# A three-stage kernel on one core: where the attention scores stand among a tile's products, and which banks hold its tables and state products

## The chip, the core and the metric

The kernel runs on one core of one Trainium2 chip. Five engines work side by side, each through its own list of instructions in order: TensorE (PE; its weight loads are PEld in the profile), VectorE (DVE), ScalarE (ACT), GpSimd (POOL) and SyncE (SP), which here issues most of the DMAs. An instruction starts when its engine has finished the one ahead of it and when the semaphores that it waits for have been raised. The metric is the device time of one execution in microseconds (us); the median of a few runs is compared.

## What is computed

Three stages follow each other: a linear attention with a decaying state, a mixture of eight experts with one expert per token, and a dense layer pair with x - tanh(x) between.

```python
def _attn_ref(r, k, v, w, u):                     # B,H,S,D = 4, 8, 768, 48
    for t in range(S):
        cur = einsum('bhd,bhe->bhde', u * k[t], v[t])
        y[t] = einsum('bhd,bhde->bhe', r[t], state + cur)
        state = w * state + einsum('bhd,bhe->bhde', k[t], v[t])

def _moe_ref(x, w_gate, w1, w2):                  # N=3072, D=384, E=8, F=1024
    probs = softmax(x @ w_gate); e = argmax(x @ w_gate)
    out = probs[e] * (relu(x @ w1[e]) @ w2[e])    # per token

def _moe2_ref(x, w_in, w_out):                    # 384 -> 2048 -> 384
    h = x @ w_in
    return (h - tanh(h)) @ w_out
```

## The kernel before

**Attention, tile by tile.** The 768 steps are cut into 6 chunks c of 128 steps; with 4 batches b this gives 24 tiles, `seq = [(c, b), ...]`, numbered n = 0 to 23. A tile holds 8 heads of 48, as 4 pairs j of two heads q. For one tile the kernel does:

- `load`: two DMAs on SP bring `n_b[n % 5]` (r, k, v by step, 576 KB) and `t_b[n % 5]` (r and k by dimension, 384 KB). There are five buffers of each, so the loads of tile n+5 wait until tile n has been used up.
- `side`: POOL makes `rk` = r*k, `rku` = rk*u and `kh` (k times a table).
- `diag_sum`: DVE sums `rku` over a head into `dt`; `diag`: ACT writes eight 128x128 diagonal matrices from it into the tile `am`.
- `scale`: DVE multiplies both halves of `t_b` by powers of the decay, one table for each half. The first, `PRKp[0]`, lies in PSUM (tag K). The second, `PRKp[1]`, lies in PSUM (tag X) for the first four tiles; `scale_rows` copies it to the SBUF tile `PRK1`, and later tiles read it there.
- `scores`: PE multiplies k and r into two banks, `A0` and `A1`, of which there is one each. `mask`: DVE copies the causal part from the banks into `am`.
- `outp`: PE multiplies r with the state of the chunk before (the **state part**, L418), adds `am` times v (the **v part**, L423) in `yh0` and `yh1`, and ACT copies both to `y`.
- `state_mm`: PE makes the state products into `Pp`, a part of the bank `yh2`; `state_add`: DVE adds them to the decayed state (`sw`, POOL), L402. Neither is needed in the last chunk.

**The gate** follows some tiles behind, once for each chunk of four: `logits` and `logits2` (PE), `gate` (nine small DVE operations and one ACT exponential), `rank_mm`, `rank_of`, `rank_in`, `rank_q`, `rank_row`, `idx_mm`: they find each token's expert and its place. Their small results share one PSUM bank, `sm`. `at_step(n, first, fn)` runs `fn` for a chunk `first` steps after the tile number that ends it. **The output** `xout(n - 7)` transposes a finished tile on PE into the bank X, scales it on ACT (`xout_g`) and writes it to `xd` in DRAM by SP; `XOUT` changes this for the last steps.

**The order** is written out by hand in the loop over n, and every engine's list follows it. In step n stand: loads of tile n+3, `diag_sum(n+1)`, `scale(n+1)`, `logits`, the output of an older tile, `outp(n-1)`, `state_mm(n)`, `diag(n+1)`, `scores(n)`, `mask(n)`, `state_add(n)`, `side(n+2)`, and the gate's parts. So scores(n) stand behind the v part of tile n-1 on PE, and on SP the loads of step n+1 stand behind the write to `xd` of step n.

**After the loop.** For the tokens of the first expert a head start is made: `head_gather` (POOL, step 22) fetches 256 rows of `xd` by an index list, as soon as the outputs of tiles 0 to 15 have landed there; `head_trans` (L610) is the first PE work after the loop's last v part, and from there on PE goes through the experts' products and the dense stage. The kernel's first lines of the loop that matter here:

```python
            if 1 <= n <= NN:
                outp(n - 1)
                at_step(n, 6, rank_row)
            if n > 1 and n < NN:
                state_mm(n)
```

Of the kernel before, what the change touches and what calls it, by code (L numbers as in the profile page):

```python
# [30 lines left out]
def rwkv_moe_moe_kernel(ctx: ExitStack, tc: tile.TileContext, rk_t, rkv, pk, u, wp1, wp2, out):  # L31


    nc = tc.nc
# [175 lines left out]
    PRK1 = ap_.tile([PT, HP, P], F32, name="PRK1")  # L210
# [7 lines left out]
    Pb = yh[2]  # L218
    Pp = Pb[:, 0:HP * D].rearrange("p (j d) -> p j d", d=D)
# [139 lines left out]
    def diag(n):  # L359
        dt = st.pop(("dt", n))  # L360
        am = at3.tile([P, 2, HP, P], F32, tag="am", name="am")
        for h in range(H):
            nc.scalar.activation(out=am[:, h % 2, h // 2, :], in_=ident, func=ACTF.Copy, scale=dt[:, h:h + 1])  # L363
        st["am", n] = am
# [43 lines left out]
    def outp(n):  # L408
        c, b = seq[n]
        am = st.pop(("am", n))  # L410

        if c > 0:
            for i in range(2):
                for g in range(2):
                    for q in range(2):
                        rows = slice(64, PT) if q else slice(0, 64)
                        j, p0 = 2 * i + g, 64 * g
                        nc.tensor.matmul(Yp[q][p0:p0 + D, i, :], lhsT=Sc[c % 2][b][rows, j, :],  # L418
                                         rhs=t_b[n % NB][rows, 0, j, :], start=(i == 0), stop=False)
        for q in range(2):  # L420
# [18 lines left out]
    PRKp = [ps1.tile([P, HP, P], F32, tag=tag, name=f"prk{tag}")[0:PT] for tag in "KX"]  # L439
# [23 lines left out]
    def gate(c):  # L463

# [5 lines left out]
        ex = exs[c % 2]  # L470
        nc.scalar.activation(out=ex[:, :, 0:E], in_=sh, func=ACTF.Exp)
        ssum = gp.tile([P, B], F32, tag="ssum", name="ssum")
        gt = gp.tile([P, B], F32, tag="gt", name="gt")
        nc.vector.scalar_tensor_tensor(out=scp, in0=sh, scalar=0.0,
# [4 lines left out]
        nc.vector.tensor_reduce(out=ssum, in_=ex, axis=AX.X, op=ALU.add)  # L479
        oh = OH[:, c]  # L480
        nc.vector.tensor_tensor(out=oh, in0=scp, in1=bc(mx.unsqueeze(2), [P, B, E]), op=ALU.is_equal)
        nc.vector.reciprocal(out=gt, in_=ssum)
        st["gt", c] = gt
        nc.vector.tensor_reduce(out=s4p, in_=oh.rearrange("p b e -> p e b"), axis=AX.X, op=ALU.add)
        nc.vector.tensor_tensor(out=cum[c + 1], in0=cum[c], in1=s4p, op=ALU.add)
        if H0 <= c < C - 1:
            nc.vector.tensor_tensor(out=cums[c + 1 - H0], in0=cum[c + 1], in1=bump16, op=ALU.add)

# [97 lines left out]
    def keep_warm(k):  # L586

        for _ in range(k):
            nc.tensor.matmul(yb[2][:, 3 * P:], lhsT=ident, rhs=ident, start=True, stop=True)
# [119 lines left out]
    with tc.manual_schedule():  # L709
# [44 lines left out]
        XOUT = {NN - 3: (NN - 10, NN - 9), NN - 2: (), NN - 1: (NN - 8, NN - 7), NN: ()}  # L754
        for n in range(NN + 1):
# [14 lines left out]
            with_logits = n % B == 1 and n > B  # L770
# [7 lines left out]
            if n > 1 and n < NN:  # L778
                state_mm(n)
            if xs_of and with_logits:  # L780
                xout_t(xs_of[0])
            if xs_of:
                xout_g(xs_of[0])
            if 0 < n < NN - 1:
                diag(n + 1)
            if n < NN:
                scores(n)
                for m in xs_of[1:]:
                    xout_t(m)
                    xout_g(m)  # L790
                mask(n)
                if n == 0:
                    k_rows()
                    diag(1)
                elif n == 1:
                    state(0)
                    state(1)
                else:
                    state_add(n)
# [6 lines left out]
            at_step(n, 3, logits2)  # L806
            at_step(n, 3, gate)
            at_step(n, 6, idx_mm)
            if n == H0 * B + 3:
                head_count()  # L810
            at_step(n, 4, rank_mm)
            at_step(n, 4, rank_of)
            at_step(n, 5, rank_in)
            if n == H0 * B + 3:
                head_end()
# [5 lines left out]
            if n == 1:  # L821
                scale_rows()
# [689 lines left out]
```

## Time and profile before

| | |
|---|---|
| time, median of 3 runs | 772.89 us (771.71 to 773.98) |
| the profiled execution's own time | 772.78 us |
| its span, first to last instruction | 771.1 us |
| PE busy in the span | 755.7 us (98%) |
| DVE busy | 639.2 us (83%) |
| ACT busy | 509.1 us (66%) |
| POOL busy | 430.9 us (56%) |

The attention loop takes about the first 118 us of the span, the rest belongs to the experts and the dense layers. A busy share says how much of a stretch had an instruction of that engine running; it doesn't say what the engine would need at its fastest, and for PE, whose matmuls overlap, it is the starts of consecutive groups that tell how long a group holds the engine.

### The profile page before, as it was taken

The numbers are of one execution on the slowest core, as the hardware profiler recorded it, in microseconds if no ns is written. First come the engines' busy times: TensorE is split into PE (matmuls) and PEld (weight loads), VectorE is DVE, ScalarE is ACT, GpSimd is POOL, SyncE is SP. The second block draws the span as 40 slices with busy tenths as digits, with TensorE's granted clock in tenths as the row PEclk, the third lists the DMA queues.
The fourth block names the chain that finished last, engine by engine and source line by source line (L and its number), as shares of the span: only waits on it lengthen the run. The fifth ranks groups of instructions, "written<-read, shape, count | busy, mean of one in ns | idle before, by whom it ended". The sixth has DMA issues, their size and how long they took to land.

```text
span 771.1 us, 14624 instructions
## 1 busy us (share of the span) xinstructions
PE 755.7 (98%) x5200; PEld 684.6 (89%) x5200; DVE 639.2 (83%) x1155; ACT 509.1 (66%) x1091; POOL 430.9 (56%) x435
## 2 busy tenths in 40 slices
PE   8899989999999999999999999999999999999997
PEld 7688868998999999999898998989989989899887
DVE  7899996788899888964898888888888888888893
ACT  6788885464454445554887766776777677677881
POOL 6989952385877876765355353443534344343433
PEclk9999999999999999999999999999999999999999
DMA  8999945466999899974000010000001000000101
GB/s 238 261 291 290 318 128 167 145 189 201 256 230 271 223 305 286 250 198 144 1 1 0 1 42 1 0 21 21 1 1 42 1 1 24 18 1 1 41 1 42
DMA packets 34656, 89.67 MB, mean 116 GB/s; under 512 B 5499, under 2 KB 12704, under 8 KB 34578
## 3 DMA queue, kind: packets, MB, share of 16 engines
q1 hardware_dynamic: 30384, 78.68, 34.8%
q0 software_dynamic: 4192, 9.99, 4.6%
q8 instruction: 43, 0.70, 0.4%
q14 instruction: 35, 0.29, 0.1%
q10 hardware_dynamic: 2, 0.00, 0.0%
HBM read 72.92 MB, written 15.74 MB: 115 GB/s over the span
## 4 chain that ended last, share of the span: by engine, by line
PE 51%; issue 2%; ACT 1%; POOL 1%; POOLq 0%
PE h L1346 25%; PE o L1394 24%; PE y L1119 1%; PE hps L1094 1%; POOL out_dram L1407 0%; PE o L1346 0%; POOL g L1383 0%; POOLq L1453 0%; POOL xb L1383 0%; ACT s L1354 0%; ACT mk L1356 0%; POOLq L1507 0%; ACT xb L1382 0%; ACT z L1350 0%; ACT t L1352 0%
## 5 line engine op out<-in xcount | busy, mean ns | idle before, releaser
L1383 POOL TENSOR_TENSOR g<-t,g 128x512 fp32r<-128x512 f32 x93 | 120.3, 1294 | 178.6 <-ACT g L1382 128.5
L1346 PE MATMUL h<-xb,ring 128*128 128x512 f32 x855 | 213.6, 395 | 0.0
L1394 PE MATMUL o<-ring,g 128*128 128x384 f32 x1116 | 209.3, 336 | 0.0
L1394 PEld LDWEIGHTS o<-ring,g 128*128 128x128 f32 x1116 | 196.1, 188 | 8.2
L1346 PEld LDWEIGHTS h<-xb,ring 128*128 128x128 f32 x855 | 159.7, 188 | 30.5
L85 POOL TENSOR_TENSOR ring<-stg,ring 128x384 fp32r<-128x384 f32 x102 | 105.3, 1053 | 53.8 <-ACT ring L84 42.4
L1350 ACT ACTIVATE z<-h 128x512 f32<-128x512 f32 x95 | 56.9, 599 | 95.2 <-PE h L1346 95.2
L1119 PE MATMUL y<-h,ring 128*128 128x256 f32 (+7 forms) x576 | 114.2, 342 | 0.6 <-DVE h L1098 0.6
L1094 PE MATMUL hps<-xt,ring 128*128 128x472 f32 (+6 forms) x504 | 105.6, 353 | 0.1
L1119 PEld LDWEIGHTS y<-h,ring 128*128 128x128 f32 x576 | 101.3, 188 | 4.1 <-DVE h L1098 1.0
L1362 DVE TENSOR_TENSOR t<-t,h 128x512 f32<-128x512 f32 x95 | 65.1, 685 | 41.3 <-ACT t L1352 40.9
L1094 PEld LDWEIGHTS hps<-xt,ring 128*128 128x128 f32 x504 | 90.6, 188 | 3.7 <-DVEq L1233 0.4
L1367 DVE COPY_PREDICATED t<-mk,h 128x512 f32<-128x512 uint32 x95 | 71.4, 751 | 10.1 <-DVE h L1365 0.5
L84 ACT CAST ring<-stg 128x384 fp32r<-128x384 f32 x152 | 70.2, 512 | 9.5 <-DMA stg<-in_wp_dram 8.9
L1364 DVE SCALAR_TENSOR_TENSOR h<-s,h 128x512 f32<-128x512 f32 x95 | 66.2, 697 | 10.6 <-ACT g L1382 0.9
L1097 ACT ACTIVATE h<-hps 128x256 fp32r<-128x256 f32 (+7 forms) x64 | 32.1, 501 | 63.8 <-PE hps L1094 61.8
L1354 ACT ACTIVATE s<-z,gb 128x512 f32<-128x512 f32 x96 | 69.6, 725 | 0.0
L1356 ACT ACTIVATE mk<-z,gt 128x512 f32<-128x512 f32 x96 | 69.3, 721 | 0.0
L1365 DVE SCALAR_TENSOR_TENSOR h<-z,h 128x512 f32<-128x512 f32 x95 | 66.1, 696 | 3.3
L1363 DVE TENSOR_TENSOR h<-h,z 128x512 f32<-128x512 f32 x95 | 65.9, 693 | 0.0
L1382 ACT CAST g<-t 128x512 fp32r<-128x512 f32 x93 | 57.6, 619 | 9.7 <-DVE t L1367 7.8
L363 ACT ACTIVATE am<-ident,dt 128x128 f32<-128x128 f32 x192 | 58.6, 392 | 3.8 <-DVE dt L356 3.8
(254 smaller groups left out, 1039.6 us busy)
## 6 DMA issues: line engine op xcount, KB each, us to landing
stg<-in_wp_dram SPq DMA_DIRECT2D x64, 384.0 KB, 4.9
n<-in_rkv_dram SPq DMA_DIRECT2D x24, 576.0 KB, 6.0
d<-in_wp_dram SPq DMA_DIRECT2D x32, 384.0 KB, 5.8
t<-in_rk_t_dram SPq DMA_DIRECT2D x24, 384.0 KB, 7.1
wdec<-dcf SPq DMA_DIRECT2D x32, 192.0 KB, 5.3
xd<-xs SPq DMA_DIRECT2D x24, 192.0 KB, 3.9
stg<-wdec SPq DMA_DIRECT2D x12, 384.0 KB, 4.3
wl<-wdec SPq DMA_DIRECT2D x2, 768.0 KB, 6.0
```

Source lines behind the costliest of these rows:

```text
L84: nc.scalar.copy(out=dst[:, 0, sl], in_=of)
L85: eng.tensor_tensor(out=dst[:, 1, sl], in0=of, in1=dst[:, 0, sl].bitcast(F32), op=ALU.subtract)
L1094: nc.tensor.matmul(ps, lhsT=wf(a, kk), rhs=xt[e][b][:, kk, :], start=(n == 0), stop=(n == 8))
L1119: nc.tensor.matmul(yps[d], lhsT=wf(a)[:, d * P:(d + 1) * P], rhs=h2[:, b, :], start=(f == 0 and n == 0), stop=(f == CH1 - 1 and n == 2))
L1346: nc.tensor.matmul(ps, lhsT=wf(a, kk), rhs=xb[j][:, b, kk, :], start=(n == 0), stop=(n == 8))
L1354: nc.scalar.activation(out=s, in_=z, func=ACTF.Square, scale=G_K ** 0.5, bias=gb)
L1356: nc.scalar.activation(out=mk, in_=z, func=ACTF.Relu, scale=-1.0, bias=gt2)
L1364: nc.vector.scalar_tensor_tensor(out=ps, in0=s, scalar=G_K * G_D, in1=ps, op0=ALU.add, op1=ALU.mult)
L1365: nc.vector.scalar_tensor_tensor(out=ps, in0=z, scalar=G_A, in1=ps, op0=ALU.subtract, op1=ALU.mult)
L1367: nc.vector.copy_predicated(out=t, mask=mk.bitcast(U32), data=ps)
L1383: nc.gpsimd.tensor_tensor(out=g[:, 1, :], in0=ww, in1=g[:, 0, :].bitcast(F32), op=ALU.subtract)
L1394: nc.tensor.matmul(ops[q], lhsT=gg[i][:, b, q * P:(q + 1) * P], rhs=wf(a), start=(f == 0 and n == 0), stop=(f == CH2 - 1 and n == 2))
```

## The change

1. Both decay tables stay in PSUM: `PRKp[1]` moves to the bank `yb[2]` (`yh2`), `PRK1` and `scale_rows` go, and `scale` reads `PRKp[k]` for all tiles.
2. The state products `Pp` move from `yh2` to free columns (304 to 496) of `sm`, the bank of the gate.
3. `outp` is split. In step n PE now does the state part of tile n-1, then scores(n), then the gate's products, then the v part of tile n-1, then the state products, then the output's transposes.
4. `diag` is split: five of the eight diagonal matrices ahead of the copies of `y`, three behind. The output of the older tile goes to the end of the step.
5. `gate` is split so that its order on DVE differs (the sum and reciprocal last), and the outputs of tiles 13 to 17 are spread over other steps (`XOUT`).
6. The products that keep PE busy at the start write to the bank X.

```diff
-    PRK1 = ap_.tile([PT, HP, P], F32, name="PRK1")
...
-        for k, by in enumerate((PRKp[0], PRKp[1] if n < B else PRK1)):
-            nc.vector.tensor_tensor(out=t[:, k], in0=t[:, k], in1=by, op=ALU.mult)
-
-    def scale_rows():
-        nc.scalar.copy(out=PRK1, in_=PRKp[1])
+        for k in range(2):
+            nc.vector.tensor_tensor(out=t[:, k], in0=t[:, k], in1=PRKp[k], op=ALU.mult)
...
+    def diag(n, part=range(H)):
+        if 0 in part:
+            st["am", n] = at3.tile([P, 2, HP, P], F32, tag="am", name="am")
+        dt, am = st["dt", n], st["am", n]
+        for q, j in (divmod(k, HP) for k in part):
+            h = 2 * j + q
+            nc.scalar.activation(out=am[:, q, j, :], in_=ident, func=ACTF.Copy, scale=dt[:, h:h + 1])
...
+    PRKp = [t.rearrange("p (j t) -> p j t", t=P)[0:PT] for t in (ps1.tile([P, BANK], F32, tag="K", name="prk"), yb[2])]
+    Pp = sm[:, 304:304 + HP * D].rearrange("p (j d) -> p j d", d=D)
...
-        XOUT = {NN - 3: (NN - 10, NN - 9), NN - 2: (), NN - 1: (NN - 8, NN - 7), NN: ()}
+        XOUT = {NN - 4: (NN - 11, NN - 10), NN - 3: (NN - 9,), NN - 2: (), NN - 1: (NN - 8, NN - 7), NN: ()}
...
-            at_step(n, 2, logits)
...
-            if xs_of and not with_logits:
-                xout_t(xs_of[0])
-            if 1 <= n <= NN:
+            ahead = range(1, NN - 1)
+            if n:
+                outp_state(n - 1)
+            if n < NN:
+                scores(n)
+                mask(n)
+            if n in ahead:
+                diag(n + 1, range(5))
+            at_step(n, 2, logits)
+            at_step(n, 3, logits2)
+            if n == H0 * B + 3:
+                head_count()
+            at_step(n, 4, rank_mm)
+            for m in xs_of[1:]:
+                xout_t(m)
+                xout_g(m)
+            if n:
                 outp(n - 1)
                 at_step(n, 6, rank_row)
...
+            if n in ahead:
+                diag(n + 1, range(5, H))
...
+            elif n < NN:
+                state(n)
+            at_step(n, 3, gate_top)
+            at_step(n, 3, gate_exp)
+            at_step(n, 3, gate_sum)
+            at_step(n, 4, rank_of)
+            at_step(n, 5, rank_in)
...
+            for m in xs_of[:1]:
+                xout_t(m)
+                xout_g(m)
```

PE, in step 14: before, the end of tile 13's state part (L418), its v part (L423), the state products of tile 14 (L390) and the first of its scores (L372).

```order
L418 MATMUL yh_162<-t_128,Sc_148 48x128
L423 MATMUL yh_161<-am,n_133 48x128 x4
L423 MATMUL yh_162<-am,n_133 48x128 x4
L390 MATMUL yh_163<-n_134,kh_160 64x48
L390 MATMUL yh_163<-n_134,kh_160 48x48
L390 MATMUL yh_163<-n_134,kh_160 64x48
L390 MATMUL yh_163<-n_134,kh_160 48x48
L390 MATMUL yh_163<-n_134,kh_160 64x48
L390 MATMUL yh_163<-n_134,kh_160 48x48
L390 MATMUL yh_163<-n_134,kh_160 64x48
L390 MATMUL yh_163<-n_134,kh_160 48x48
L372 MATMUL A_1393<-t_129 128x128
```

PE, the same step of the changed kernel (line numbers are its own): the end of tile 13's state part (L411), the scores of tile 14 (L367), the gate's second products (L460) and tile 13's v part (L420).

```order
L411 MATMUL yh_161<-t_128,Sc_148 48x128
L367 MATMUL A_1356<-t_129 128x128
L367 MATMUL A_1357<-t_129 128x128
L367 MATMUL A_1356<-t_129 128x128
L367 MATMUL A_1357<-t_129 128x128
L367 MATMUL A_1356<-t_129 128x128
L367 MATMUL A_1357<-t_129 128x128
L367 MATMUL A_1356<-t_129 128x128
L367 MATMUL A_1357<-t_129 128x128
L460 MATMUL sm<-sel,lt 128x8 x4
L420 MATMUL yh_160<-am,n_133 48x128 x4
L420 MATMUL yh_161<-am,n_133 48x128 x4
```

The scores moved from behind the v part and the state products to ahead of both.

ACT, in step 21: before, the logits' copy (L455), the two copies of `y` (L428), a gate operation (L546), an output (L577), the eight diagonals of tile 22 (L363), the output of tile 15 (L577) and a cast of weights.

```order
L455 COPY lt<-lps 128x512
L428 COPY y<-yh_161 128x2x128
L428 COPY y<-yh_162 128x2x128
L546 ACTIVATE rh<-hv,pid 128x4x32
L577 ACTIVATE xs<-Xps,gt 128x384
L363 ACTIVATE am<-ident,dt 128x128 x8
L577 ACTIVATE xs<-Xps,gt 128x384
L84 CAST ring_70<-stg 128x384
```

ACT, the same step of the changed kernel.

```order
L359 ACTIVATE am<-ident,dt 128x128 x5
L454 COPY lt<-lps 128x512
L425 COPY y<-yh_160 128x2x128
L425 COPY y<-yh_161 128x2x128
L561 ACTIVATE rh<-hv,pid 128x4x32
L359 ACTIVATE am<-ident,dt 128x128 x3
L592 ACTIVATE xs<-Xps,gt 128x384
L84 CAST ring_70<-stg 128x384
```

Five diagonals moved ahead of the copies, and the step's last output stands behind all eight. In the steps between, before, the one output stands ahead of the eight diagonals; now it stands behind them there too.

## Rows read from the trace of the kernel before

**Rows 1.** Busy time per engine by stretch; columns in the first line.

```profile
core 0: us, PE busy (x) PEld busy (x) DVE busy (x) ACT busy (x) POOL busy (x), PEclk, DMA share, GB/s
78.25:95.96 17.71, 17.58 (x317) 14.27 (x315) 17.43 (x43) 15.85 (x50) 16.26 (x19) 1.00 1.02 314
```

**Rows 2.** DVE's groups, shapes apart, 0 to 130 us: busy us, mean ns.

```profile
L328 DVE TENSOR_TENSOR t<-t,PRK 112x512 f32<-112x512 f32 x20 | 20.3, 1015 | 0.0
L328 DVE TENSOR_TENSOR t<-t,prkK 112x512 f32<-112x512 f32 x24 | 16.2, 677 | 0.0
```

**Rows 3.** Waits between 28 and 118 us: total us, times, longest.

```profile
PEld yh L423 <- DVE am L377: 7.0, 19, 1.3
...
PE yh L423 <- DVE am L377: 4.2, 5, 1.7
...
DVE am L377 <- PE A L372: 2.0, 3, 1.3
```

**Rows 4.** PE in order of time: start us, us, engine, line, form, count.

```profile
82.06 0.61 PE L390 MATMUL yh<-n,kh 128*64 128x48 f32 x16
82.61 1.16 PE L372 MATMUL A<-t 64*128 64x128 f32 x16
83.70 1.07 PE L452 MATMUL lps<-y,wgp 128*32 128x512 f32 x8
84.70 0.66 PE L418 MATMUL yh<-t,Sc 64*48 64x128 f32 x16
85.28 1.08 PE L423 MATMUL yh<-am,n 128*48 128x128 f32 x16
86.19 0.61 PE L390 MATMUL yh<-n,kh 128*64 128x48 f32 x16
```

**Rows 5.** POOL in order of time; tiles 8 and 22.

```profile
38.25 1.00 POOL L342 TENSOR_TENSOR rku<-rk,ub 128x384 f32<-128x384 f32 x1
...
99.26 1.00 POOL L336 TENSOR_TENSOR rk<-n 128x384 f32<-128x384 f32 x1 [0.67 <-DMA n<-in_rkv_dram]
100.34 1.00 POOL L342 TENSOR_TENSOR rku<-rk,ub 128x384 f32<-128x384 f32 x1
```

**Rows 6.** DVE in order of time: a gate's first operation, sums of tiles 8 and 22.

```profile
41.51 0.17 DVE L467 TENSOR_REDUCE m<-sm 128x4 f32<-128x32 f32 x1
...
42.95 0.55 DVE L356 TENSOR_REDUCE dt<-rku 128x8 f32<-128x384 f32 x1
...
106.22 0.55 DVE L356 TENSOR_REDUCE dt<-rku 128x8 f32<-128x384 f32 x1
```

**Rows 7.** ACT in order of time, step 21.

```profile
105.37 0.56 ACT L455 COPY lt<-lps 128x512 f32<-128x512 f32 x1
105.83 0.71 ACT L428 COPY y<-yh 128x256 f32<-128x256 f32 x2
...
107.28 2.44 ACT L363 ACTIVATE am<-ident,dt 128x128 f32<-128x128 f32 x8
109.62 0.57 ACT L577 ACTIVATE xs<-Xps,gt 128x384 f32<-128x384 f32 x1
```

**Rows 8.** SP's DMA issues in order of time, and the page's issue groups (last number: us to landing).

```profile
92.17 0.34 SPq L580 DMA_DIRECT2D xd<-xs  x1
92.61 0.37 SPq L238 DMA_DIRECT2D n<-in_rkv_dram  x1
...
110.21 0.32 SPq L580 DMA_DIRECT2D xd<-xs  x1
...
n<-in_rkv_dram SPq DMA_DIRECT2D x24, 576.0 KB, 6.0
```

**Rows 9.** The end of the loop: POOL's gather, PE's first transposes of it.

```profile
115.45 0.96 POOL L599 DMA_INDIRECT n<-xd,idxh  x1 [0.30 <-issue]
...
119.84 0.77 PE L610 MATMUL hp<-ident,n 128*128 128x128 f32 x5 [0.64 <-DMA n<-xd,idxh]
```

**Rows 10.** Busy time by stretch, as in rows 1, early in the loop.

```profile
28.00:32.00 4.00, 4.00 (x48) 3.61 (x45) 2.80 (x11) 2.77 (x10) 3.92 (x5) 0.57 1.01 253
```

More of the change, by code (lines that the diff above doesn't have):

```diff
@@ L357, in diag_sum @@
         st["dt", n] = dt
[L359 to L364, printed above, removed]
+    def diag(n, part=range(H)):
[5 more added lines that the diff above has]
+            nc.scalar.activation(out=am[:, q, j, :], in_=ident, func=ACTF.Copy, scale=dt[:, h:h + 1])
     def scores(n):
@@ L419, in outp @@
                                          rhs=t_b[n % NB][rows, 0, j, :], start=(i == 0), stop=False)
+    def outp(n):
+        c, b = seq[n]
+        am = st.pop(("am", n))
         for q in range(2):
@@ L437, in x_bank @@
         return ps1.tile([P, HP, P], F32, tag=tag, name=name)
-    PRKp = [ps1.tile([P, HP, P], F32, tag=tag, name=f"prk{tag}")[0:PT] for tag in "KX"]
+    PRKp = [t.rearrange("p (j t) -> p j t", t=P)[0:PT] for t in (ps1.tile([P, BANK], F32, tag="K", name="prk"), yb[2])]
+    Pp = sm[:, 304:304 + HP * D].rearrange("p (j d) -> p j d", d=D)
+    warm = ps1.tile([P, HP, P], F32, tag="X", name="warm")
     pqp, ipqp, iplp = (sm[0:PT, 32 * k:32 * k + 32].rearrange("p (j a) -> p j a", a=8) for k in range(3))
@@ L463, in gate, with gate_top, gate_diff @@
     def gate(c):
+        gate_diff(c)
+        gate_exp(c)
+        gate_hot(c)
+        gate_sum(c)
+    def gate_top(c):
+        gate_diff(c)
+        gate_hot(c)
+    def gate_diff(c):
         lg = sm[:, 128:128 + 8 * B].rearrange("p (b e) -> p b e", e=E)
@@ L469, in gate, with gate_exp, gate_hot @@
         nc.vector.tensor_tensor(out=sh, in0=lg, in1=bc(m.unsqueeze(2), [P, B, E]), op=ALU.subtract)
[L470 to L474, printed above, removed]
+        st["sh", c] = sh
+    def gate_exp(c):
+        nc.scalar.activation(out=exs[c % 2][:, :, 0:E], in_=st["sh", c], func=ACTF.Exp)
+    def gate_hot(c):
+        nc.vector.scalar_tensor_tensor(out=scp, in0=st["sh", c], scalar=0.0,
                                        in1=e8p.unsqueeze(1).to_broadcast([P, B, E]),
@@ L487, in gate, with gate_sum @@
             nc.vector.tensor_tensor(out=cums[c + 1 - H0], in0=cum[c + 1], in1=bump16, op=ALU.add)
+    def gate_sum(c):
+        ssum = gp.tile([P, B], F32, tag="ssum", name="ssum")
+        gt = gp.tile([P, B], F32, tag="gt", name="gt")
+        nc.vector.tensor_reduce(out=ssum, in_=exs[c % 2], axis=AX.X, op=ALU.add)
+        nc.vector.reciprocal(out=gt, in_=ssum)
+        st["gt", c] = gt
     def head_count():
@@ L588, in keep_warm @@
         for _ in range(k):
-            nc.tensor.matmul(yb[2][:, 3 * P:], lhsT=ident, rhs=ident, start=True, stop=True)
+            nc.tensor.matmul(warm[:, 0], lhsT=ident, rhs=ident, start=True, stop=True)
     HD = HEAD // P
@@ L766, in rwkv_moe_moe_kernel @@
                 scale(n + 1)
-            at_step(n, 2, logits)
             at_step(n, 6, rank_q)
             xs_of = [m for m in XOUT.get(n, (n - LAG,)) if m >= 0]
-            with_logits = n % B == 1 and n > B
             if n == NN - 1:
                 st["both"] = True
-            if xs_of and not with_logits:
-                xout_t(xs_of[0])
-            if 1 <= n <= NN:
+            ahead = range(1, NN - 1)
[15 more added lines that the diff above has]
+            if n:
                 outp(n - 1)
                 at_step(n, 6, rank_row)
[L778 to L799, printed above, removed]
+            if n in ahead:
+                diag(n + 1, range(5, H))
+            if n == 0:
+                k_rows()
+                diag(1)
+            elif n == 1:
+                state(0)
+                state(1)
+            elif n < NN:
[5 more added lines that the diff above has]
+            at_step(n, 5, rank_in)
+            if n == H0 * B + 3:
+                head_end()
+            for m in xs_of[:1]:
+                xout_t(m)
+                xout_g(m)
             if n + 2 < NN:
```

18 lines of the change are left out of this document (1 added, 17 removed).

## Prediction

> **What bounds the kernel now.** I looked first at the chain that ended last: it is PE from the experts to the end, so whatever the attention loop gives back at its end should come off the total one for one. Then I read the loop stage by stage with the busy time by stretch. In a set of four tiles, 17.71 us long, DVE is busy for 17.43, PE for 17.58, and the DMA engines are at 1.02 of their share [rows 1]. Three resources are therefore near their limit together, and a change that relieves one of them can't be credited with the whole of what it removes.
>
> The groups of DVE's instructions say what is avoidable there: `scale` with the SBUF table takes 1015 ns against 677 with the table in PSUM, the shapes being equal [rows 2]. The waits show the coupling of the two engines: PE waits for the mask, DVE for the scores [rows 3].
>
> The row that matters most is a lag. POOL had tile 8's `rku` ready at 39.25 us (start 38.25 plus 1.00) [rows 5]; DVE began to sum it at 42.95 [rows 6], 3.7 us late, since it was busy with older work. For tile 22 the two times are 101.34 and 106.22, a lag of 4.9. POOL itself follows the loads: for tile 22 it waits for a DMA [rows 5]. So DVE trails the supply of data by some 4 us all through the loop, and that lag is the credit which a faster DVE can collect; what comes in behind it is the loads' pace.
>
> **The tables.** 20 multiplications become 0.338 us shorter, 20 x (1.015 - 0.677) = 6.8 us of DVE [rows 2]. In the stretch of four tiles that is 1.4 us, so DVE's need falls to about 16.1 of 17.7. The copy of the table on ACT goes too, at no time that anybody waits for.
>
> **The scores ahead of the v part.** Before, from mask to mask PE had the v part, the state products and the scores to do, 0.91 + 0.55 + 1.09 = 2.55 us by the starts of the groups [rows 4], besides the transposes. Now only the scores, 1.09, stand between two masks. DVE's waits for the scores (2.0 us) and most of PE's waits for the mask (4.2 us as matmuls) [rows 3] lose their cause. But PE has the same instructions as before. One tile costs it 0.55 + 1.09 + 0.58 + 0.91 [rows 4] and the transposes, and a set of four with the gate's products fills 17.58 of 17.71 us by the busy time [rows 1]. Its own need lies between 4 x 3.13 + 1.0 = 13.5 (these rows alone, without transposes and the gate's later products) and 17.6; I take 17.3, near the upper end, because the starts of its groups stand without a gap. So the pace between tile 8 and tile 22, 3.5 sets, can improve by at most 0.4 us a set, 1.4 in all.
>
> **The loads' way.** Here the change adds something. On SP the loads of the next step stand behind the write of an output, and that output now stands on ACT behind all eight diagonals of the next tile instead of ahead of them. From the start of a sum on DVE: 0.55 to the first diagonal, five diagonals 1.46 (2.34 us to the next start for eight), two copies 0.7, three diagonals 0.88, the output 0.57 [rows 7], then 0.44 from the write's issue to the load's [rows 8]: 4.6 us. Then 6.0 to landing [rows 8], 2.1 for POOL's two products [rows 5], and the sum of the tile three further on can start. A lap of three tiles thus takes 12.7 us. Each lap meets one step's extra ACT work; the logits' copy holds ACT for 0.46 [rows 7], and I add 0.24 a lap for it and its like. 12.95 us for three are 17.3 for four: just what PE needs, and below 17.7. Before, the output stood ahead of the diagonals and this loop had room.
>
> So the pace becomes 17.3 to 17.7 a set. With the lag of 3.7 us collected at tile 8 and 0 to 0.9 from the pace, the sum of tile 22 starts 3.7 to 4.9 us earlier (the upper end is the lag there, since the tile's own load hardly moves). I take 4.2, nearer to the lower end, as the pace hardly moves.
>
> **The state products in the gate's bank.** The same products, written elsewhere. DVE's small gate operations and PE's state products now share `sm`; a wait between them would hold PE for one gate's block, 42.95 - 41.51 = 1.44 us [rows 6], once a set, some 7 us in five. I cost it at nothing: the gate stands behind `state_add` on DVE, and PE has transposes, a state part, scores and a v part to do before it writes the bank again (0.58 + 1.09 + 0.91 us without the transposes [rows 4]), longer than the block. The other bound is a gain: `yh2` is no longer written by PE, which can free nothing that anyone waited for, so 0. The Trainium skill speaks against such sharing: "PSUM — Partial Sum Buffer", section "PSUM bank collisions raise a hardware error", says that the chip doesn't hold two engines apart that touch one bank in the same partitions, so that semaphores must guard by bank. By that rule every gate operation and every state product has to be ordered, whichever columns they use; no row of before shows state products and gate in one bank, and the price would be the 1.44 us a set just given, if the order fell badly.
>
> **The end of the loop.** The head start's gather needs the output of tile 15 in DRAM. Before, ACT began this output at 109.62, 3.40 us after the sum of tile 22 [rows 6, 7]; its write went out at 110.21 [rows 8], and PE got the rows at 119.84 after a wait [rows 9]. Now ACT has, from the same sum: 0.55, five diagonals 1.46, the logits' copy 0.46, two copies 0.6, a small operation 0.4, three diagonals 0.88, hence 4.35 us, 0.95 later. The gather's 9.6 us from write to use are latency and don't shrink. So the gather comes 4.2 - 0.95 = 3.25 us earlier, while the last v part comes about 4.5 earlier, and PE's wait for the gather grows from 0.64 to about 2. What is late next is the gather, and it sets the result.
>
> **The sum.** The profiled execution took 772.78 us (span 771.1 and 1.7 around it), 0.1 under the median of the runs. 772.78 - 3.25 = 769.5 us.
>
> **Rivals.**
> - *The whole credit passes.* If the gather is no bound (its index or its write earlier than I think) and the pace reaches PE's 17.3, the gain is the lag of 4.9 and 0.9 from the pace: 767.0, range 766.2 to 768. For it: DVE's 6.8 us and the waits; against it: a wait for the gather stands already [rows 9]. Chance 0.14.
> - *The end gives it back.* PE waits 2 us for the gather. After a wait of up to 1.7 us [rows 3] the granted clock fell early in the loop: 0.57 in the mean of 28 to 32 us [rows 10], 1.2 instead of 2.4 GHz for most of it, which loses 4 x 0.43 = 1.7 us of PE. Once behind the gather wait, where PE sets the end, that makes 771.2; with a pace of 17.7 added, 772. Range 771 to 774. Against it: before, the shorter waits at this place cost no clock. Chance 0.27.
> - *Slower: the loads' lap.* The lap of three tiles is level with the old pace at 17.7 x 3/4 = 13.28 us, that is at 6.3 us to landing. The median is 6.0, but tile 22's load took 6.65 from issue to POOL's start (92.61 to 99.26) [rows 5, 8]. Each further microsecond costs 1.33 a set and about 4.7 over 3.5 sets. At 6.65 the gain shrinks to some 1.2 us; from 6.9 on the kernel is slower than before; at 7.5 it takes 775.6. Place: POOL's r*k products waiting for `n`, DVE's sums behind them, all through tiles 11 to 22. For it: the DMA engines are at 1.02 of their share [rows 1], and the changed kernel asks for the same bytes in less time. Against it: loads issued later are also less crowded. Chance 0.10, 774 to 778.
> - *The shared bank.* PE's state products wait for gate blocks: five times 1.44 us against the gain, 776.7 at worst, from the point where PE reaches them within 1.7 us of the last ones. Chance 0.05.
> - *It doesn't do what it says:* the table in PSUM being no faster. The row with 24 multiplications at 677 ns [rows 2] runs beside the same POOL work, so I give it no chance of its own.
>
> **How the numbers follow.** Forecast 0.44, 768 to 771; the rivals as given. A measurement of this kernel can tell about 0.3%, 2.3 us, from no change. Faster by more (under 770.5): 0.14 and most of the forecast, 0.37, makes 0.51. Within: the rest of the forecast, 0.07, the second rival, 0.27, and a little of the others, 0.02, makes 0.36. Slower: 0.13. The range leaves out the upper half of the slower cases and half of the fastest ones: 766.8 to 774.5.
>
> **What would show it.** Right: all `scale` rows near 0.68 us; DVE with gaps in the middle of the loop, ended by POOL's `rku`, and the lag at tile 8 below 1 us; PE's waits for the mask gone; the last mask 4 to 5 us earlier than before, but the first transpose of the gathered rows only about 3, with a longer wait for the DMA in front. Wrong: sets of four tiles longer than 17.7 us with POOL waiting for loads (the lap), PE's state products waiting for a gate operation (the bank), or a stretch of granted clock near 0.5 after the gather. If the gather isn't waited for at all, the tail was mis-sized and the gain is larger.

## The result, and the profile after

The changed kernel took 781.19 us in the median against 772.68 for the kernel before, a ratio of 1.0109 (95% interval 1.0078 to 1.0141); beside the later experiments, 1.0069 (1.0040 to 1.0098). The forecast was 769.5, and its range ended at 774.5. The profiled execution took 779.45 us with a span of 777.6, 6.6 more than before.

What the change was meant to do is in the trace. DVE's groups, shapes apart, 0 to 130 us (the answer to [rows 2]):

```profile
L325 DVE TENSOR_TENSOR t<-t,yh 112x512 f32<-112x512 f32 x24 | 16.3, 679 | 0.0
L325 DVE TENSOR_TENSOR t<-t,prk 112x512 f32<-112x512 f32 x24 | 16.2, 676 | 0.0
```

The waits between 28 and 118 us (the answer to [rows 3]) no longer hold PE's wait for the mask, and DVE waits for scores once; other waits stand in their place:

```profile
ACT am L359 <- DVE dt L350: 13.5, 14, 1.9
POOL rk L330 <- DMA n<-in_rkv_dram: 12.8, 9, 2.7
...
DVE idf L573 <- PE sm L568: 3.1, 3, 1.9
...
PE Xps L585 <- ACT lt L454: 2.4, 3, 1.0
...
PE Xps L585 <- ACT xs L592: 2.0, 1, 2.0
...
DVE am L372 <- PE A L367: 0.9, 1, 0.9
```

Busy time by stretch, columns as in [rows 1]: two sets of four tiles from the sum of tile 12 to that of tile 20, and a short stretch later in the loop:

```profile
59.36:78.26 18.90, 18.15 (x312) 15.00 (x310) 16.52 (x44) 15.28 (x48) 14.86 (x18) 1.00 0.87 273
78.26:97.65 19.39, 18.60 (x327) 15.41 (x325) 17.10 (x44) 15.80 (x49) 14.80 (x18) 1.00 0.94 290
106.31:109.71 3.40, 3.40 (x37) 2.61 (x40) 2.45 (x5) 2.65 (x9) 2.29 (x4) 0.50 0.93 297
```

A set takes 18.9 us where it took 17.7, with DVE 0.9 us less busy. PE, busy for 17.58 of 17.71 us before [rows 1], now stands still for 0.75 of 18.90: part of the time has gone into waits between engines.

Behind the loop the first expert's gather is late as well. POOL's first gather and PE's first wait for its rows, in order of time:

```profile
149.12 0.94 POOL L1085 DMA_INDIRECT xg<-xd,idx  x1 [12.10 <-DVE tok L982]
...
159.41 0.45 PE L1096 MATMUL tps<-ident,xg 128*128 128x128 f32 x2 [1.56 <-DMA xg<-xd,idx]
```

The places in the loop are read from the starts of DVE's sums of tiles 4, 8, 20 and 22 and of PE's first transposes of the gathered head rows. Before, tiles 4 and 20 (the others stand in [rows 6, 9]):

```profile
24.54 0.55 DVE L356 TENSOR_REDUCE dt<-rku 128x8 f32<-128x384 f32 x1 [0.56 <-POOL rku L342]
...
96.69 0.54 DVE L356 TENSOR_REDUCE dt<-rku 128x8 f32<-128x384 f32 x1
```

In the changed kernel:

```profile
22.64 0.55 DVE L350 TENSOR_REDUCE dt<-rku 128x8 f32<-128x384 f32 x1 [0.28 <-POOL rku L336]
...
40.11 0.52 DVE L350 TENSOR_REDUCE dt<-rku 128x8 f32<-128x384 f32 x1
...
97.65 0.55 DVE L350 TENSOR_REDUCE dt<-rku 128x8 f32<-128x384 f32 x1
...
106.79 0.55 DVE L350 TENSOR_REDUCE dt<-rku 128x8 f32<-128x384 f32 x1
...
123.65 1.03 PE L625 MATMUL hp<-ident,n 128*128 128x128 f32 x6
```

The last row names no wait: when PE comes to the head rows, they are there. The second of its six transposes, from which the table below counts in every kernel, starts at 123.91.

The 6.6 us by place, from the starts in the two traces: the sum of tile 8 comes at 40.11 instead of 42.95, **-2.8**; the three sets to tile 20 are 1.65, 1.20 and 0.94 longer, **+3.8**; from the sum of tile 20 to PE's first full use of the gathered head rows [rows 9] 26.26 instead of 23.15, **+3.1**; from there to the end 653.7 instead of 651.2, **+2.5**. The first of these, the gain, was 0.9 short of the credit that the prediction wanted to collect; of the losses it had only 0.95 at the loop's end.

### The profile page after: what moved, and what is told of

It reads as the page before. It is cut to its first block, busy times and chain, and to the rows that moved or that the text cites. A ratio compares the mean times of both kernels' runs of the same rounds, so it can differ in the third digit from the quotient of the medians.

```text
span 777.6 us, 14622 instructions
## 1 busy us (share of the span) xinstructions
PE 759.3 (98%) x5200; PEld 688.4 (89%) x5200; DVE 637.1 (82%) x1155; ACT 506.9 (65%) x1090; POOL 424.2 (55%) x435
## 4 chain that ended last, share of the span: by engine, by line
PE 51%; issue 2%; ACT 1%; POOL 1%; POOLq 0%
PE h L1361 25%; PE o L1409 23%; PE y L1134 1%; PE hps L1109 1%; POOL out_dram L1422 0%; PE o L1361 0%; POOL g L1398 0%; POOLq L1468 0%; POOL xb L1398 0%; ACT mk L1371 0%; ACT s L1369 0%; POOLq L1522 0%; ACT xb L1397 0%; ACT z L1365 0%; ACT t L1367 0%
## 5 line engine op out<-in xcount | busy, mean ns | idle before, releaser
L1112 ACT ACTIVATE h<-hps 128x256 fp32r<-128x256 f32 (+7 forms) x64 | 32.0, 500 | 67.2 <-PE hps L1109 61.4
L359 ACT ACTIVATE am<-ident,dt 128x128 f32<-128x128 f32 x192 | 61.0, 392 | 17.2 <-DVE dt L350 17.1
L1397 ACT CAST g<-t 128x512 fp32r<-128x512 f32 x93 | 57.6, 619 | 8.5 <-DVE t L1382 6.5
```

## Experiments

The table holds for each kernel the ratio to the kernel before in the same session and, from its profiled execution (us): the start of tile 8's sum, the set from the sum of tile 12 to that of tile 16, PE's first full use of the head rows, and what is left from there to the end.

| kernel | ratio (95%) | sum 8 | set | head rows | rest |
|---|---|---|---|---|---|
| before | 1 | 42.95 | 17.70 | 119.84 | 651.2 |
| changed | 1.0109 (1.0078 to 1.0141) | 40.11 | 18.90 | 123.91 | 653.7 |
| e11, changed again | 1.0069 (1.0040 to 1.0098) | 40.51 | 18.91 | 123.81 | 652.9 |
| e1 2 KB back | 1.0041 (1.0017 to 1.0065) | 40.81 | 18.90 | 122.36 | 651.2 |
| e2 + loads early | 1.0037 (1.0016 to 1.0058) | 43.88 | 18.91 | 125.99 | 651.7 |
| e4 slow table | 1.0105 (1.0064 to 1.0146) | 39.97 | 20.25 | 127.05 | 651.2 |
| e8 slow table, own bank | 1.0093 (1.0063 to 1.0123) | 40.12 | 19.55 | 125.05 | 651.2 |
| e5 logits' copy first | 1.0081 (1.0052 to 1.0109) | 42.49 | 18.92 | 128.08 | 651.7 |
| e6 + index later | 1.0080 (1.0055 to 1.0105) | 42.05 | 18.56 | 123.44 | 651.2 |
| e7 + loads early | 1.0069 (1.0045 to 1.0092) | 42.85 | 18.56 | 126.90 | 651.2 |
| e10 = e6, split at 2 | 1.0033 (1.0009 to 1.0058) | 40.21 | 18.62 | 120.92 | 651.8 |
| e13 = e10 + loads early | 1.0051 (1.0023 to 1.0079) | 41.50 | 17.93 | 121.27 | 651.7 |
| e14 + index first | 1.0173 (1.0146 to 1.0200) | 40.38 | 22.91 | 132.69 | 650.8 |
| e3 old order, tables, bank | 1.0371 (1.0332 to 1.0409) | 42.56 | 24.97 | 150.18 | 651.2 |
| e9 = e3, products late | 1.0010 (0.9984 to 1.0036) | 39.88 | 19.47 | 120.28 | 651.1 |
| e12 = e9, index later | 0.9986 (0.9956 to 1.0017) | 39.55 | 19.96 | 120.59 | 651.3 |

Several profiled executions hold a stretch of 3.4 us or more at half clock in the loop, which shifts all that follows, so differences of 1 to 2 us in the head rows are not read. The set of the table is free of such stretches except in e3 and e14, where the granted clock in it is 0.91 and 0.85, which makes some 2.2 and 3.4 us of it. There is one profile of each kernel; where two ran the same code, tile 8 differs by 0.4 us (changed and e11) and 0.8 (e6 and e7). The set alone doesn't give the time either: e9's is longer than the changed kernel's, and e9 is level with the kernel before.

**e1: the tile of 2 KB back.**

```
+    pad = ap_.tile([PT, HP, P], F32, name="pad")     # never used
     ipw = ap_.tile([PT, HP, 17], F32, name="ipw")
```

> The changed kernel with an unused tile of 2 KB a partition put back where the SBUF table stood, so that every later tile has the address that it had before the change; nothing else is touched. Theory L (layout): in the changed kernel the first expert's gather buffers overlap the attention's small tiles by the missing 2 KB, and the gather waits for DVE (149.12 us, 4.8 us later than the 4.16 us by which the stage had slipped explain), which costs PE about 2.4 us. Then the gather returns to some 4.2 us behind that of before, and the time falls by 2.4 to about 777.0. The loop stays as it is (first transpose of the gathered head rows near 123.6). Rival: the gather is late because of the work in front of it; the time stays within 0.7 of 779.5.

The gather, from the trace of e1:

```profile
142.62 0.94 POOL L1086 DMA_INDIRECT xg<-xd,idx  x1 [7.23 <-DVE bt L945]
```

It stands 20.27 us behind the first use of the head rows (before: 20.28; changed: 25.21), and the rest is 651.2 us again. Theory L holds: 2.5 us of the loss have nothing to do with what the change computes. Removing `PRK1` moved the pools behind it down by 2048 bytes. Why that delays the gather is argued, not shown. By a reckoning of the addresses, which no view here holds, the gather buffers had lain wholly on the buffers of Y, which are free early, and now the last of the four reaches 96 bytes into the pool of the gate's small tiles; that already the first gather waits would mean that the pool is held as a whole.

> The changed kernel once more, beside e9 and e10 on one chip, to compare with e1_pad (1.0041): the profile prices the layout at 2.5 us (651.2 us from the first use of the gathered rows to the end with the tile of 2 KB in place, 653.7 without), which is 0.003 of the time. Expected 1.007 to 1.011.

1.0069 against e1's 1.0041 is a price of 0.0028, 2.2 us, but the intervals overlap; the price stands on the traces, which give 1.8 (e11) to 2.5 (changed).

**e2: the loads ahead of the output.**

```
-            if n + 3 < NN: load(n + 3)          # head of the step
+            if n + 4 < NN: load(n + 4)          # behind outp(n - 1), ahead of xout
```

> As e1_pad, and in each step the next load is issued ahead of the output's write on SP's queue (it waits only for its buffer, which the v part of the tile before frees). Theory P (loads' lap): the sets of four tiles in the loop take 18.9 to 19.4 us since the load stands behind the output, which stands behind all eight diagonals. Taken ahead of it, loads go out at least 1 us earlier a tile, POOL stops waiting for them, sets fall to 17.3 to 17.7 us, and the time to 770 to 773. Rival O (order of the engines): DVE, PE and ACT wait for one another in the new order and loads are late only because the steps are; then sets stay at 18.9 or more and the time within 1 us of e1_pad, 776 to 778.

POOL's wait for loads between 45 and 98 us, e1 and then e2, and e2's set:

```profile
POOL rk L331 <- DMA n<-in_rkv_dram: 10.0, 7, 2.4
```

```profile
POOL rk L331 <- DMA n<-in_rkv_dram: 1.2, 3, 0.5
```

```profile
62.91:81.82 18.91, 18.17 (x312) 15.00 (x310) 16.52 (x43) 15.30 (x48) 15.11 (x19) 1.00 0.87 272
```

The waits went and the set stayed to 0.01 us; the time is e1's. The lap of the loads, the prediction's own slower rival, is visible in the changed kernel and does not by itself set its pace. (Tile 8 is later in e2: its loads ask for tile 4 at 5.8 us, among the first ones, and its profile holds a half-clock stretch from 30.5 us.)

**e3 and e9: the tables without the order.** e3 is the old order with both tables in PSUM and the state products in `sm` (points 1, 2 and 6 of the change); e9 moves the state products behind the scores and the gate's products.

```
     def scale(n): ... in1=PRKp[k]                  # e3: k = 0 and 1, both PSUM
     Pp = sm[:, 304:304 + HP * D] ...               # e3
-            if n > 1 and n < NN: state_mm(n)       # e9: from ahead of the scores
+                    logits2; head_count; rank_mm; idx_mm; state(n)   # e9: behind the mask
```

> The kernel before with both tables in PSUM and the state products in the gate's bank, in the old order, with the 2 KB kept as an unused tile: the first and third part of the change alone. If the tables are worth what the DVE rows say, the sum of tile 8 starts up to 3.7 us earlier and the time is 768.5 to 771. If the shared bank costs (PE's state products waiting for gate operations, 1.44 us a set), the time is 774 to 777. If loads set the pace of the old order too, it stays within 1 us of 772.8.

> As e3_tables (the old order, both tables in PSUM, the state products in the gate's bank), but each tile's state products stand behind its scores and behind the gate's products, right ahead of the sum that reads them. Theory B (bank): e3 lost its time because products of the gate that stood between the state products and their sum had to wait for DVE to read the bank; with nothing between them the waits go, and the time falls by 25 us or more, to 770 to 775. Theory W (PE is the bound of the old order too, at 17.75 us a set) adds: not below 769.5, since faster tables relieve only DVE. If another cost of the tables or of the bank was behind e3, it stays above 785.

e3's waits up to 140 us:

```profile
PE sm L458 <- DVE Sc L397: 6.9, 4, 1.7
...
PE sm L550 <- DVE Sc L397: 5.0, 3, 1.7
PE sm L501 <- DVE Sc L397: 4.9, 3, 1.7
```

These are the logits' second product, the index and the rank products. None uses what DVE's state sum `Sc` reads; they write other columns of the same bank, and each time PE stands for 1.7 us until the sum, which follows the mask on DVE, has read it. The loop is 30 us longer, far beyond all three times that were expected; eight half-clock stretches, 34 us together, make up to 17 of the 30. With nothing between the products and their sum (e9) the loss is gone: 1.0010. Theory B holds. The Trainium skill, "PSUM — Partial Sum Buffer", section "PSUM bank collisions raise a hardware error", says that semaphores have to guard PSUM by bank and quadrant of partitions, in the simple version by bank, and not by address. The waits of these rows, on products in other columns, agree.

So the tables and the shared bank need one thing of the order, the state products right ahead of their sum. They don't need the scores ahead of the v part: e9 has them behind it, as before. It gains nothing either. Its tile 8 comes 3.1 us earlier and its way from the sum of tile 20 to the head rows is 1.9 shorter, but its three sets from tile 8 to tile 20 take 59.2 us instead of 53.7.

Part of that is the same bank at another pair, the state products behind DVE's read of the index sums, between 45 and 98 us:

```profile
PE sm L385 <- DVE idf L555: 2.4, 2, 1.2
```

**e4 and e8: the order without the tables.**

```
-            nc.vector.tensor_tensor(out=t[:, k], in0=t[:, k], in1=PRKp[k], ...)
+            ... in1=(PRKp[0], PRKp[1] if n < B else PRK1)[k] ...      # e4, e8
+    Pp = yh[2][:, 0:HP * D]; PRKp in banks K and X                   # e8
```

> The changed kernel with the second table read from SBUF from tile 4 on, as before (the tile of 2 KB is in use again): the new order and the shared bank without the faster tables. DVE has 0.34 us more a tile from tile 4 on. Theory P (the load lap sets the pace, DVE has slack): the time is that of e1_pad, 776 to 778. Rival O (DVE is in the loop that sets the pace): each tile costs up to 0.34 more, 20 tiles 3 to 6.8 us, so 780 to 784.

> As e4_order (the new order, the second table read from SBUF), and the state products are back in a bank of their own, the tables in the banks of before: the new order alone. If sharing the gate's bank costs nothing in the new order (the products stand right ahead of the sum that reads them, and no PE row of the changed kernel waits for DVE there), the time is that of e4_order, 780 to 784, 1% above before. If the bank is what made the set longer, sets fall to 17.7 and the time to 772 to 775.

The sets, e4 and then e8:

```profile
59.96:80.21 20.25, 18.99 (x312) 15.49 (x310) 18.34 (x43) 15.39 (x48) 16.12 (x18) 1.00 0.80 249
```

```profile
59.17:78.73 19.56, 18.76 (x313) 15.42 (x310) 18.45 (x44) 15.29 (x48) 16.44 (x19) 1.00 0.84 265
```

The three sets from tile 8 to tile 20, which no half-clock stretch touches in these traces, take 53.7 us before, 58.8 in e8, 61.4 in e4 and 57.6 in e1. The order alone thus costs 5.1 us of them, the shared bank 2.6 more, and the fast table gives back 3.8, of the 4.1 that 12 tiles save DVE. DVE's queue is part of what sets the pace, and theory P falls here too: the ratios of e4 and e1 are 0.0064 apart. Those of e4 and e8 can't be told apart, so the time is that of e8's first reading (the shared bank costs nothing in the new order), but it couldn't show 2.6 us either; this price of the bank stands on one trace of each alone.

The times put the loss where it belongs. The tables and the bank without the new order cost nothing (e9, 1.0010); the new order without them costs 0.9% (e8, 1.0093); with both it is 0.4% (e1), and 0.7 to 1.1% where the layout comes on top (the changed kernel). "Order" here is all that e8 has, points 3 to 5 of the change; they were not run apart.

**e5, e6, e10: PE's waits, one after the other.** On ACT: the logits' copy ahead of the diagonals (e5); the index products one step later, behind the scores (e6); two diagonals instead of five ahead of the copies of Y (e10).

```
+            at_step(n, 2, logits)                        # e5: from behind diag
+            at_step(n, 7, rank_row)                      # e6: was step 6, behind outp
-                diag(n + 1, range(5))
+                diag(n + 1, range(2))                    # e10; the other six behind outp
             at_step(n, 3, logits2)
+            at_step(n, 7, idx_mm)                        # e6: was step 6, end of the step
```

> As e1_pad, and on ACT the logits' copy out of the X bank stands ahead of the first five diagonals instead of behind them. Theory W (PE is the bound, with the starts of its groups without a gap, and a set of four grew from 17.75 to 18.95 us by waits on PE's own queue: 0.77 between the state products and the output's transposes, which wait for the logits' copy to leave the single X bank; 0.27 of index products; the rest seams of 0.02 to 0.08): the 0.77 becomes 0, the set 18.2 us, the time 2 to 2.5 below e1_pad. Rival: DVE's order sets the pace (its queue holds state sums and index sums that wait for PE); then PE waits elsewhere, sets stay at 18.9 and the time that of e1_pad.

> As e5_logits, and the index products of the first three chunks stand one step later, directly behind the scores, with the small operation on ACT that feeds them ahead of the diagonals. Theory W: PE's 0.49 for them falls to 0.22 as before the change and DVE's wait for them goes; sets of 17.9 us, the time 3 to 4 below e1_pad, level with before or 1 under it. Rival: as for e5_logits, sets stay at 18.5 or more.

> As e6_logits_idx, with two diagonals ahead of the copies of Y on ACT and six behind them, in place of five and three. In e6 PE's state part waits for these copies (0.45 us a set between the output's transposes and the state part), and the copies stand behind diagonals that wait for DVE's sum. Theory R (ring through ACT): the wait goes, the set falls from 18.6 to 18.0 or below, the time 1.5 to 3 below e6. Rival: the last diagonals, now 0.9 us later, hold the mask, and the set stays at 18.6 or grows.

PE's set of four, split by the time from the first product of a group to the first of the next, shows where the waits stand (us, one set in the middle of the loop):

| group | before | changed | e5 | e6 | e10 | e13 | e9 |
|---|---|---|---|---|---|---|---|
| scores | 4.37 | 4.37 | 4.37 | 4.37 | 4.88 | 4.71 | 4.37 |
| state part | 2.55 | 2.68 | 2.67 | 2.94 | 2.34 | 2.34 | 2.34 |
| v part | 3.84 | 3.64 | 3.64 | 3.64 | 4.19 | 3.67 | 4.04 |
| state products | 2.18 | 2.94 | 2.18 | 2.18 | 2.23 | 2.23 | 2.38 |
| output's transposes | 2.28 | 2.36 | 3.13 | 2.80 | 2.35 | 2.34 | 2.35 |
| logits, both | 1.91 | 1.99 | 1.99 | 1.91 | 1.91 | 1.91 | 1.99 |
| ranks | 0.36 | 0.43 | 0.44 | 0.44 | 0.44 | 0.44 | 0.44 |
| index | 0.22 | 0.49 | 0.49 | 0.28 | 0.28 | 0.28 | 1.56 |
| set | 17.72 | 18.90 | 18.91 | 18.56 | 18.62 | 17.92 | 19.46 |

In the changed kernel 0.76 of the 1.18 stand behind the state products. The rows are these, PE, ACT and DVE in order of time:

```profile
88.41 0.61 PE L385 MATMUL sm<-n,kh 128*64 128x48 f32 x16
...
89.15 0.56 ACT L454 COPY lt<-lps 128x512 f32<-128x512 f32 x1
...
89.76 0.66 PE L585 MATMUL Xps<-ident,y 128*128 128x128 f32 x4 [0.73 <-ACT lt L454]
...
90.36 0.56 PE L568 MATMUL sm<-rh,ol 128*128 128x32 f16 x8
...
90.96 0.19 DVE L573 TENSOR_TENSOR idf<-idf,sm 128x32 f32<-128x32 f32 x1 [0.65 <-PE sm L568]
```

The transposes wait for the logits' copy to leave the single X bank, and DVE then waits for the index products behind them. e5 takes that wait away, and 0.77 stand behind the transposes instead, ahead of the index products; the trace puts them down to DVE's state sum in the shared bank. e6 takes that away, and the state part waits for the copies of Y on ACT. e10 takes that away, and the scores and the v part take 0.5 longer each, with no wait of PE there that the trace names. The set moved from 18.90 by 0.3 in all. Each expectation named its wait rightly and missed the set: one ring of waits (engines that wait for one another in a circle) lay under the other.

The times say a little more than this one set. e5 and e6 are no faster than e1 but rather slower (1.0081 and 1.0080 against 1.0041). e10 is below e6 by more than its expectation said, 1.0033 against 1.0080, and its tile 8 comes 1.8 us earlier. Over all three sets from tile 8 to tile 20, e1 takes 57.6 us, e6 56.2, e10 55.8 and e13, which follows, 54.8, against 53.7 before.

**e7 and e13: the loads once more.** The same edit in both, from step 8 on: the load of n + 4 ahead of the output, on top of e6 and of e10.

> As e6_logits_idx, and from step 8 on the loads stand ahead of the output's write on SP's queue. In e2 this took POOL's waits for loads away (10.0 to 1.2 us) and changed no pace. With PE's waits gone the loads may be next: by the working of the prediction a lap of three tiles is 12.95 us, 17.3 a set, below 17.9. Theory W: within 1 us of e6_logits_idx. If the loads' lap is what then binds, 1.5 to 3 us faster than e6_logits_idx.

> As e10_split2, and from step 8 on the loads stand ahead of the output's write on SP's queue. In e10 the sums of tiles 11, 13, 15 and 19 start within 0.3 us of POOL's product, and POOL waits 9.2 us for loads between 45 and 98 us. Theory P2 (with the ring through ACT cut, the loads' lap is what is left): POOL's waits go, the sets fall from 18.6 to 18.0 or below, the time 1.5 to 2.5 below e10. Rival D (DVE's queue, with the waits for state products and index sums in it, sets 18.6): POOL's waits go as in e2, and the sets stay within 0.2 of 18.6.

The set of e10 and of e13:

```profile
58.17:76.79 18.62, 18.24 (x312) 14.95 (x310) 16.70 (x43) 15.42 (x49) 15.00 (x19) 1.00 0.90 279
```

```profile
59.45:77.38 17.93, 17.93 (x312) 14.80 (x310) 16.43 (x44) 15.38 (x49) 15.70 (x19) 1.00 0.99 294
```

On e6 the edit changes nothing (18.56 both times); on e10, with the ring through ACT cut, it takes 0.7 off this set, and POOL's waits for loads between 45 and 98 us fall from 9.2 to 3.4 us. So the loads' lap was there, one layer below, and for the set theory P2 holds. In e13 PE is busy for all of the 17.93 us, 0.2 above the old order's 17.70. That is not yet the least the new order could take: the smallest entries of the table's rows, changed to e13, add up to 17.5, an estimate that no run reached. The time does not show the shorter set (1.0051 against 1.0033, intervals overlapping): e13's profile holds a half-clock stretch ahead of tile 8, and its way from the sum of tile 20 to the head rows is 24.9 us as in e10, 1.8 more than before.

**e14 and e12: the index products ahead of the scores.**

```
+            at_step(n, 7, rank_row); at_step(n, 7, idx_mm)   # e14, on e13: ahead of scores(n)
+            at_step(n, 7, idx_mm)                            # e12, on e9: ahead of scores(n)
```

> As e13_split2_loads, and the index products stand ahead of the scores, so that DVE's index sum stands ahead of the mask and the state products no longer wait for it in the shared bank (0.4 us of PE a set in e10). Rival D: the set falls by 0.3 to 0.5 from e13's. Theory P2: no more than 0.2. If both hold, sets of 17.7 and a time level with before or 1 us under it, 771 to 774.

> As e9_tables_late, and the index products of the first three chunks stand one step later and ahead of the scores, so that the state products no longer wait for DVE to read the index sums out of the shared bank. In e9 that is 1.56 us a set between the index products and the state products on PE, against some 0.2. Theory B (every pair of bank users that stand close on two engines costs a wait): the sets fall from 19.4 to 18.0 or 18.3, the first use of the gathered head rows from 120.3 to 116 or 117, and the time to 768.5 to 771: faster than before by 0.2 to 0.5%. Theory W (PE or the gather sets the end anyway): the sets fall, but the gather of the head rows is then waited for, and the time stays at 771 to 773.

Both missed. In e14 PE waits at the index products for the small operation on ACT (2.0 us in two, between 45 and 98 us), and the set grows to 22.9, of which some 3.4 are half-clock; that DVE's index sum ahead of the mask passes the wait on is argued from the order. In e12 the wait of e9 went, but the set of the table holds 1.6 us ahead of a v part for which the trace shows nothing waited for; the other two sets are 18.9 and 19.0, not 18.0. Its time is the kernel before's.

## Why the prediction was wrong

In the prediction's own terms: the sum of tile 22 was to start 4.2 us earlier and starts 0.57 later, which is 4.8 of the miss; from there to the head rows it was to take 0.95 longer than the 13.62 us of before and takes 17.12, which is 2.55; and 2.5 are the layout. Together that is the distance from 3.25 us faster to 6.6 slower. The step that failed is the first, the pace of the loop. (The prediction's 1.4 us at most from the pace, 3.5 sets of 0.4, also stands as 0 to 0.9 in its sum; the forecast doesn't hang on it.)

**The tables: the duration right, the credit wrong.** The 0.338 us a tile is there. The prediction read the lag of 3.7 us at tile 8 [rows 5, 6] as DVE's debt, to be paid by faster tables. e4 and e8, with the slow table, start tile 8's sum at 39.97 and 40.12, as early as the changed kernel. So the gain of 2.8 at tile 8 does not need the faster tables. The traces place it: 1.9 are there at the sum of tile 4 (24.54 to 22.64), ahead of the first multiplication that reads another table, and their cause is open. The other 0.9 lies between tiles 4 and 8, where the profile of before holds the half-clock stretch of [rows 10]; e13 and e10, the same code up to step 8, differ there by 0.9 too (18.47 against 17.55 us), and e13 has such a stretch. So that part may well be the clock of one execution; no profile of before without the stretch was kept that could show it. The lag, which was to fall below 1 us, is 2.1: POOL's `rku` of tile 8 is ready at 38.03.

**The scores ahead of the v part: this step failed.** "I take 17.3": the waits of [rows 3] did go, but the set did not fall, it grew to 18.9. That the order is the cause is shown by e8 (1.0093 with nothing else changed) and e9. The term took the pace to be what PE needs, and that is where it failed. PE's own need is not the main part: the new order ran at 17.9 (e13), and its groups at their shortest add up to 17.5. About 1.0 us a set is waits between engines that the new order made, and they lie in at least two layers: one ring through ACT (sum on DVE, five diagonals and the logits' copy on ACT, copies of Y, PE's state part and scores, back to DVE), which e5, e6 and e10 cut step by step for 0.3 of this set, and the loads' lap, for 0.7, which shows only once that ring is cut. The prediction costed the moved instructions on ACT only for the way of the loads, and never the wait of PE's transposes for the X bank, though the diff puts the logits' copy behind five diagonals, 1.46 us by its own working [rows 7].

**The loads' lap: named as a rival, seen, and not the cause.** The sign that was asked for, sets longer than 17.7 with POOL waiting for loads, is there in full. e2 takes the waits away and leaves the set, and so does e7. What the sign showed was steps that came late for another reason. The lap decides only from 18.6 downwards, once the ring through ACT is cut (e13).

**The shared bank: costed at nothing.** Between 28 and 118 us no PE row of the changed kernel waits more than 0.2 us for it, yet e4 less e8 is 0.7 to 0.9 us a set by the trace, though not by the time, and users of the bank wait for one another in e5, e9 and e10. The large waits were not those of the rival, in which gate operations hold the state products: in e3 the state sum holds the gate's products, 1.7 us each time. The rival's own pair is there in e9, 1.2 us at the index sums.

**The end of the loop.** Forecast 3.25 us earlier, measured 4.07 later. The 1.0 at tile 20 is the pace less the early gain. Of the 3.1 behind it up to 1.7 are half-clock: 3.4 us at 0.50 from 106.3, right after PE had waited 1.96 us for the X bank in step 20, in which two outputs now pass through it. In e1, the same loop without such a stretch, the way from the sum of tile 20 to the head rows is 23.96 us, only 0.8 longer than before; in e10 and e13 it is 1.8 longer, also without one there. That was not taken apart. The gather, which the prediction took for the bound, isn't: the changed kernel's PE doesn't wait for it, and e1's waits 0.42 us. PE itself comes late.

**Not in the prediction at all: 2.5 us of layout** (e1). The diff showed a tile of 2 KB leaving the pool, and the working counted only the copy into it.

Together, over the three sets: the order +5.1 (e8), the bank +2.6 (e4 less e8), the tables -3.8 (e1 less e4), which comes to the +3.8 of the changed kernel, each from one trace, and for this way of adding them one by one; the gain of 2.8 ahead of them, the end of the loop and the layout make up the rest of the 6.6.

## What to carry to other kernels

Where three engines are each near full, a wait that is taken away uncovers the next one: judge a reordering by all rings that an instruction stands in, and a visible wait as the cause only when taking it away moves the pace. A PSUM bank that two engines use was one resource here whatever the columns (e3, 1.7 us a wait): put its writer right ahead of its reader. And when a buffer leaves a pool, look at what the later pools now lie on.

## What the runs showed of the hardware

The wait of PE for the X bank in step 20 was 1.96 and 2.10 us in the two profiles of the changed kernel and 2.01 in e7, and a half-clock stretch of 3.4 us followed each within 2 us. In e1 and e10 it was 1.28 and 1.34, and the clock stayed at 1.00. But the length of this wait doesn't settle it: in e8 and e2 it was 2.28 and 2.22 us, and the clock stayed at 1.00 there too, and in e4, with 1.09, a stretch came ahead of it, from about 105 us. The rows of the wait in the changed kernel, in e1 and in e8, and e8's clock behind it:

```profile
105.68 0.66 PE L585 MATMUL Xps<-ident,y 128*128 128x128 f32 x4 [1.96 <-ACT xs L592]
```

```profile
105.74 0.66 PE L586 MATMUL Xps<-ident,y 128*128 128x128 f32 x4 [1.28 <-ACT xs L593]
```

```profile
107.73 0.66 PE L585 MATMUL Xps<-ident,y 128*128 128x128 f32 x4 [2.28 <-ACT xs L592]
```

```profile
107.00:111.00 4.00, 3.27 (x46) 1.96 (x46) 3.97 (x9) 4.00 (x13) 2.38 (x4) 1.00 0.86 268
```

Between the changed kernel and e1, whose loops are the same, the longer wait (0.7) and the half-clock stretch (1.7) account for the 2.3 us by which their ways from the sum of tile 20 to the head rows differ. In e3 eight of PE's eleven waits of 1.64 to 1.73 us behind 30 us were followed by half clock within 1.5 us, three were not, and its mean granted clock was 0.977. What else decides is open.

The spread of the times goes with the clock: over all runs of the kernel before, from 768.6 to 781.8 us, those with a mean granted clock of 1.00 took 771.8 us on average and those at 0.993 778.0.
